# Storing the last tiles of a linear-attention and MLP kernel: one two-batch transfer from SyncE's queue in place of two half transfers from two queues

## The chip, the cores and the metric

The kernel runs on one core of a Trainium2 chip. The metric is the device time of one execution in microseconds; lower is better. The kernel before takes 283.94 us, the median of three runs that lie between 283.93 and 284.04. A profiled execution took 283.87 us, and the traced part of it, the span, is 282.1 us long. All times below that are positions in the trace are counted from the start of that span.

## The reference, cut to what matters

```python
B, H, S, D = 8, 8, 576, 64          # batches, heads, sequence, head size
q, k, v: (B, H, S, D) float32       # about N(0, 0.1)
w_in: (512, 2048)    w_out: (2048, 512)

phi(x)  = where(x > 0, x, exp(x) - 1) + 1
kv      = einsum('bhsd,bhse->bhde', phi(k), v)
z       = sum over s of phi(k)
attn    = (phi(q) @ kv) / (phi(q) @ z + 1e-6)
x       = attn as (B*S, H*D) = (4608, 512)
out     = gelu_tanh(x @ w_in) @ w_out      # (4608, 512) float32
```

The output has 4608 rows of 512 float32, which is 2048 bytes per row. Batch b owns rows 576 b to 576 b + 575.

## The kernel before

A batch has 576 rows, which is four tiles of 128 and a rest of 64. The kernel runs the MLP for each batch on its first 512 rows (`MAIN`), in iterations 0 to 7. The 64 rows left over from each of the eight batches (`REST`) are collected, two batches to a tile, into four tiles of 128 rows. Iteration 8 (`j == B`) runs the MLP on them. So a tile `t` of the rest group holds 64 rows of batch 2t in partitions 0 to 63, and 64 rows of batch 2t + 1 in partitions 64 to 127. In the output these two blocks of 64 rows lie 576 rows apart.

In iterations 0 to 7, two tiles at a time are stored in one transfer from ScalarE's queue, with 128 partitions of 1024 float32. In iteration 8 each tile is evacuated from PSUM by VectorE or ScalarE in turn, and stored by two transfers, one for each batch. The last tile is computed in three column pieces of 256, 128 and 128, each with its own evacuation and its own two stores.

```python
P = 128; MAIN = 512; REST = S - MAIN          # REST = 64
pout = tile_pool(name="pout", bufs=2)         # two o_sb buffers, used in turn
# ... (cut)

def store_rest(t, o_sb, fs, engs):
    for s in range(2):
        r0 = (2 * t + s) * S + MAIN
        engs[s].dma_start(
            out=out[r0 : r0 + REST, fs], in_=o_sb[REST * s : REST * (s + 1), 0, fs]
        )

def finish(j, t, o_ps):
    if j == B:                                 # the rest group
        o_sb = pout.tile([P, 2, d_model], FP32, name="o_sb")
        evac(o_sb[:, 0, :], o_ps, t % 2)       # VectorE for even t, ScalarE for odd t
        store_rest(t, o_sb, slice(0, d_model), (nc.scalar, nc.sync))
        return
    # ... (cut: iterations 0 to 7, one store of two tiles from ScalarE's queue:)
    #     ov = out[j*S : j*S+MAIN].rearrange("(p c) f -> p c f", c=C)[:, t-1 : t+1]
    #     nc.scalar.dma_start(out=ov, in_=o_sb)

def last_tile(g, t):                           # t = 3 of the rest group
    o_sb = pout.tile([P, 2, d_model], FP32, name="o_sb")
    for n, fs in enumerate((slice(0, 256), slice(256, 384), slice(384, d_model))):
        o_ps = bank("o_ps", [P, fs.stop - fs.start])
        o_mm(o_ps, g, t, range(MM), fs)
        evac(o_sb[:, 0, fs], o_ps, n == 0)     # ScalarE, then VectorE twice
        store_rest(t, o_sb, fs, (nc.scalar, nc.sync))
```

Of the kernel before, what the change touches and what calls it, by code (L numbers as in the profile page):

```python
# [15 lines left out]
def kernel(  # L16
# [16 lines left out]
    nc = tc.nc  # L33

    B, H, S, D = q.shape
    d_model, d_ff = moe_w_in.shape
# [3 lines left out]
    MAIN = P * C  # L40
    REST = S - MAIN
# [37 lines left out]
    def bank(name, shape, dt=FP32):  # L79
        return ps_b.tile(shape, dt, name=name, tag="b")  # L80
# [421 lines left out]
    def at(j, slot, fn, *args):  # L502


        fill.setdefault((j, slot), []).append((fn, args))
# [179 lines left out]
    def evac(dst, src, on_scalar):  # L685
        (nc.scalar.copy if on_scalar else nc.vector.tensor_copy)(dst, src)  # L686

    def store_rest(t, o_sb, fs, engs):
        for s in range(2):
            r0 = (2 * t + s) * S + MAIN  # L690
            engs[s].dma_start(
                out=out[r0 : r0 + REST, fs], in_=o_sb[REST * s : REST * (s + 1), 0, fs]
            )

    o_sbs = {}

    def finish(j, t, o_ps):
        if j == B:
            o_sb = pout.tile([P, 2, d_model], FP32, name="o_sb")
            evac(o_sb[:, 0, :], o_ps, t % 2)  # L700
            store_rest(t, o_sb, slice(0, d_model), (nc.scalar, nc.sync))
            return
        if t % 2 == 0:
            o_sbs[j, t // 2] = pout.tile([P, 2, d_model], FP32, name="o_sb")
        o_sb = o_sbs[j, t // 2]
        if j == 0 and t in (1, 2):
            at(0, 35, evac, o_sb[:, t % 2, :], o_ps, True)
        else:
            evac(o_sb[:, t % 2, :], o_ps, t < C - 1 if j == 0 else t % 2)
        if t % 2 == 1:  # L710
            ov = out[j * S : j * S + MAIN, :].rearrange("(p c) f -> p c f", c=C)[:, t - 1 : t + 1]

            def store():
                nc.scalar.dma_start(out=ov, in_=o_sb)

            if j == 0:
                at(1, 2, store)
            else:
                store()

    def o_mm(o_ps, g, t, ms, fs=slice(0, d_model), half=None):
        for m in ms:
            if m == ms.start + 2 and half:
                run(*half)
            nc.tensor.matmul(  # L725
                o_ps,
                lhsT=g[:, m, P * t : P * (t + 1)],
                rhs=w_out_sb[:, m, fs],
                start=(m == 0),
                stop=(m == MM - 1),  # L730
            )

    def last_tile(g, t):
        o_sb = pout.tile([P, 2, d_model], FP32, name="o_sb")
        for n, fs in enumerate((slice(0, 256), slice(256, 384), slice(384, d_model))):
            o_ps = bank("o_ps", [P, fs.stop - fs.start])
            o_mm(o_ps, g, t, range(MM), fs)
            evac(o_sb[:, 0, fs], o_ps, n == 0)
            store_rest(t, o_sb, fs, (nc.scalar, nc.sync))

    def iteration(j):
        xt = xts[j] if j < B else xt_rest
# [12 lines left out]
        for slot, step in enumerate(steps):  # L755
            if step[0] == "h":
                m = step[1]
                h_ps = h_begun.get(j, {}).get(m)
                if h_ps is None:
                    h_ps = bank("h_ps", [P, MAIN])  # L760
                    h_mm(h_ps, xt, m)
                gelu(g, m, h_ps)
            else:
                t, u = step[1:]
                if j == B and t == C - 1:
                    if u.start == 0:
                        last_tile(g, t)
                    continue
                if u.start == 0:
                    o_pss[t] = bank("o_ps", [P, d_model])  # L770
                o_mm(o_pss[t], g, t, u, half=(j, slot - 0.5))
                if u.stop == MM:
                    finish(j, t, o_pss[t])
            run(j, slot)
# [54 lines left out]
```

## Time and profile before

| What | Value | From |
|---|---|---|
| Time, median of three | 283.94 us | the runs |
| Span of the trace | 282.1 us | the profile page |
| PE busy | 276.1 us, 98% | the page, part 1 |
| ACT, DVE, POOL busy | 164.3, 102.6, 15.0 us | the page, part 1 |
| Granted TensorE clock | 0.998 on average | the run |
| Output stores of iterations 0 to 7 | 16 of 512 KB from ScalarE's queue, 3.2 us to landing | the page, part 6 |
| Output stores of the rest group | 12, six from each queue, 128 KB to 32 KB, from 269.1 to 279.1 us | the trace, by line L691 |

PE stands for TensorE's matmuls, DVE for VectorE, ACT for ScalarE, POOL for GpSimd. SPq and ACTq are the instruction streams of SyncE and ScalarE in which transfers are issued. Lines such as L691 are lines of the kernel. In the DMA views q1 is the queue of transfers that SyncE issues and q10 that of transfers that ScalarE issues; this follows from their counts and sizes. A packet is one piece of a transfer as one of the core's 16 DMA engines moved it. "Share of 16 engines" is the sum of the packets' times over 16 times the length of the window. "Landing" is counted from the issue of a transfer to its last completion event.

### The profile page before, as it was taken

The page shows a single profiled execution, that of the slowest core. Times are in us where ns is not written, and L with a number is a line of the kernel's source. Part 1 is how long each engine was busy: PE and PEld are TensorE (multiplying, and loading weights), DVE is VectorE, ACT ScalarE, POOL GpSimd, SP SyncE. Part 2 cuts the span into 40 slices and gives each one's busy share as a digit, 9 for nine tenths or more (in the row PEclk, how much of TensorE's full clock was granted, in tenths as well). Part 3 has the DMA queues.
Part 4 walks back from the last instruction along what each step waited for, and adds up shares of the span by engine and source line. Part 5 has one row for each costly group of instructions (what it writes and reads, how often), then busy time and mean ns, then how long its engine had stood idle before and what let it go on. Part 6 is the DMA issues. An engine that isn't in the chain of part 4 may idle for free.

```text
span 282.1 us, 5465 instructions
## 1 busy us (share of the span) xinstructions
PE 276.1 (98%) x2341; PEld 135.3 (48%) x2341; DVE 102.6 (36%) x177; ACT 164.3 (58%) x224; POOL 15.0 (5%) x21
## 2 busy tenths in 40 slices
PE   8899999999999999999999999999999999999995
PEld 3474455445444544454445444544444444444444
DVE  3850386344955750356034640350124001400001
ACT  4678878786986905692569346833681364026400
POOL 3147210000000000000000000000000000000000
PEclk9999999999999999999999999999999999999999
DMA  7999999978899767916794740056405300520022
GB/s 245 401 406 397 410 402 404 404 251 222 185 379 294 263 153 212 380 26 168 188 388 114 151 131 0 2 151 168 94 2 149 114 0 2 142 81 0 2 74 74
DMA packets 59591, 53.83 MB, mean 191 GB/s; under 512 B 35760, under 2 KB 45360, under 8 KB 59568
## 3 DMA queue, kind: packets, MB, share of 16 engines
q1 hardware_dynamic: 56784, 44.58, 51.0%
q10 hardware_dynamic: 2784, 8.91, 8.7%
q8 instruction: 18, 0.29, 0.4%
q14 instruction: 5, 0.04, 0.0%
HBM read 36.70 MB, written 9.44 MB: 164 GB/s over the span
## 4 chain that ended last, share of the span: by engine, by line
PE 94%; DMA 3%; SPq 1%; DVE 1%; issue 0%; ACT 0%
PE o_ps L725 44%; PE h_ps L384 44%; DMA v_x<-in_v_dram 3%; PE n_ps L322 1%; PE n_ps L249 1%; PE kv_ps L249 1%; PE n_ps L265 1%; PE t_ps L377 1%; SPq L95 1%; SPq L100 0%; PE t_ps L530 0%; DVE vp L238 0%; DVE x L367 0%; DVE kvbd L261 0%; DVE o_sb L686 0%
## 5 line engine op out<-in xcount | busy, mean ns | idle before, releaser
L725 PE MATMUL o_ps<-w_out_sb,g 128*128 128x512 bf16 (+2 forms) x608 | 128.4, 368 | 0.0
L384 PE MATMUL h_ps<-xt,w_in_sb 128*128 128x512 bf16 (+1 forms) x564 | 113.7, 359 | 0.0
L394 ACT ACTIVATE g<-h_ps 128x512 bf16<-128x512 f32 x144 | 84.5, 599 | 36.4 <-PE h_ps L384 35.1
L384 PEld LDWEIGHTS <-w_in_sb 128*128 128x128 bf16 x628 | 58.5, 98 | 64.7
L725 PEld LDWEIGHTS <-g 128*128 128x128 bf16 x608 | 57.4, 98 | 63.5
L686 ACT COPY o_sb<-o_ps 128x512 f32<-128x512 f32 (+1 forms) x19 | 10.8, 576 | 65.7 <-PE o_ps L725 58.9
L686 DVE COPY o_sb<-o_ps 128x512 f32<-128x512 f32 (+1 forms) x19 | 12.2, 645 | 50.5 <-PE o_ps L725 45.6
L282 DVE RECIPROCAL r<-n_ps 128x6 f32<-128x6 f32 (+2 forms) x43 | 8.2, 191 | 60.9 <-PE n_ps L322 55.4
L227 DVE TENSOR_SCALAR k_p<-k_x 128x2304 bf16<-128x2304 f32 (+1 forms) x9 | 11.0, 1222 | 24.4 <-DMA k_x<-in_k_dram 24.4
L283 DVE TENSOR_TENSOR xs<-n_ps,r 128x384 bf16<-128x384 f32 (+1 forms) x30 | 17.5, 584 | 1.0
L219 ACT ACTIVATE k_e<-k_x 128x2304 bf16<-128x2304 f32 (+1 forms) x9 | 17.1, 1902 | 0.9 <-DMA k_x<-in_k_dram 0.8
L219 ACT ACTIVATE q_e<-q_x 128x2048 bf16<-128x2048 f32 (+1 forms) x9 | 15.5, 1719 | 2.8 <-DMA q_x<-in_q_dram 2.7
L227 DVE TENSOR_SCALAR q_p<-q_x 128x2048 bf16<-128x2048 f32 (+1 forms) x9 | 9.9, 1102 | 13.1 <-DMA q_x<-in_q_dram 13.1
L384 PE MATMUL h_ps<-xt_rest,w_in_sb 128*128 128x512 bf16 x64 | 14.0, 379 | 0.0
L233 DVE TENSOR_TENSOR q_p<-q_p,q_e 128x2048 bf16<-128x2048 bf16 (+1 forms) x9 | 9.9, 1100 | 6.9 <-ACT q_e L219 6.8
L407 ACT ACT_TABLE_LOAD x9 | 11.5, 1283 | 0.2
L233 DVE TENSOR_TENSOR k_p<-k_p,k_e 128x2304 bf16<-128x2304 bf16 (+1 forms) x9 | 11.0, 1221 | 1.2 <-ACT k_e L219 1.0
L238 DVE CAST vp<-v_x 128x2304 bf16<-128x2304 f32 (+1 forms) x9 | 11.0, 1223 | 0.5 <-DMA v_x<-in_v_dram 0.4
L416 PE MATMUL w_ps<-warm 128*128 128x512 bf16 x32 | 9.3, 445 | 1.2 <-DVE warm L181 1.2
L219 ACT ACT_TABLE_LOAD x8 | 10.3, 1283 | 0.1
L139 POOL CAST w_in_sb<-w_st 128x512 bf16<-128x512 f32 (+2 forms) x6 | 7.6, 1271 | 14.6 <-DMA w_st<-in_moe_w_in_dram 14.6
L283 DVE TENSOR_TENSOR x<-n_ps,r 128x512 bf16<-128x512 f32 (+1 forms) x13 | 7.9, 609 | 0.4
(50 smaller groups left out, 77.5 us busy)
## 6 DMA issues: line engine op xcount, KB each, us to landing
out_dram<-o_sb ACTq DMA_DIRECT2D x16, 512.0 KB, 3.2
k_x<-in_k_dram SPq DMA_DIRECT2D x7, 1152.0 KB, 7.2
v_x<-in_v_dram SPq DMA_DIRECT2D x7, 1152.0 KB, 11.8
q_x<-in_q_dram SPq DMA_DIRECT2D x6, 1024.0 KB, 9.6
w_st<-in_moe_w_in_dram SPq DMA_DIRECT2D x3, 1024.0 KB, 13.5
q_x<-in_q_dram SPq DMA_DIRECT2D x4, 512.0 KB, 8.5
w_st<-in_moe_w_out_dram SPq DMA_DIRECT2D x2, 1024.0 KB, 12.5
w_st<-in_moe_w_out_dram SPq DMA_DIRECT2D x4, 512.0 KB, 11.2
```

The source lines that it names most:

```text
L219: nc.scalar.activation(o, i, AF.Exp)
L227: nc.vector.tensor_scalar(o, i, 1.0, 1.0, op0=ALU.add, op1=ALU.max)
L233: nc.vector.tensor_tensor(p, p, e, op=ALU.min)
L238: fn(out=vp_paired(b)[:, :, us, 0:D].rearrange("p j u d -> p u j d"), in_=ld["v", b][:, us].rearrange("p u (j d) -> p u j d", d=D),)
L282: nc.vector.reciprocal(r, n_v[heads + (D,)])
L283: nc.vector.tensor_tensor(x_v, n_v[heads + (slice(0, D),)], r[heads + (None,)].to_broadcast(shape + [D]), op=ALU.mult,)
L384: nc.tensor.matmul(h_ps[:, ts], lhsT=w_in_sb[:, c, P * m : P * (m + 1)], rhs=xt[:, c, ts], start=(c == 0), stop=(c == KM - 1), skip_group_ ...
L394: nc.scalar.activation(g[:, m, :], h_ps, AF.Gelu_apprx_tanh)
L407: nc.scalar.preload_act_table_set("gelu_apprx_tanh_and_others")
L416: nc.tensor.matmul(w_ps, lhsT=warm[:, 0:P], rhs=warm)
L686: (nc.scalar.copy if on_scalar else nc.vector.tensor_copy)(dst, src)
L725: nc.tensor.matmul(o_ps, lhsT=g[:, m, P * t : P * (t + 1)], rhs=w_out_sb[:, m, fs], start=(m == 0), stop=(m == MM - 1),)
```

## The change

`store_rest` is rewritten. In place of a loop over the two batches, which issues one transfer of 64 partitions for each from two queues, there is a single transfer of all 128 partitions from SyncE's queue. Its destination is the output seen as batches by rows, two batches and the last 64 rows of each, so that the step between the two batches is a dimension of the access pattern. The aim is fewer issued transfers: six in place of twelve, and none of them on ScalarE's instruction stream.

```diff
-    def store_rest(t, o_sb, fs, engs):
-        for s in range(2):
-            r0 = (2 * t + s) * S + MAIN
-            engs[s].dma_start(
-                out=out[r0 : r0 + REST, fs], in_=o_sb[REST * s : REST * (s + 1), 0, fs]
-            )
+    def store_rest(t, o_sb, fs, eng):
+
+        eng.dma_start(
+            out=out.rearrange("(b s) f -> b s f", s=S)[2 * t : 2 * t + 2, MAIN:S, fs],
+            in_=o_sb[:, 0, fs],
+        )
 ... (finish)
-            store_rest(t, o_sb, slice(0, d_model), (nc.scalar, nc.sync))
+            store_rest(t, o_sb, slice(0, d_model), nc.sync)
 ... (last_tile)
-            store_rest(t, o_sb, fs, (nc.scalar, nc.sync))
+            store_rest(t, o_sb, fs, nc.sync)
```

Nothing else moves: the order of the instructions on TensorE, VectorE and GpSimd is the same in both programs, and ScalarE's and SyncE's differ only in these stores. In the built program the destination of a full tile's store has the counts 2 x 64 x 512 (outermost first), with steps of 294912, 512 and 1 elements; its source has 128 partitions of 512 elements. The stores of before have 64 x 512 on both sides.

## The prediction

> **What bounds the kernel now.** I read the page's chain first, then the chain's last stretch, then the tail in order of time, and last the DMA packets in windows of it. The chain, from the page (shares of the span by engine):
>
> ```profile
> ## 4 chain that ended last, share of the span: by engine, by line
> PE 94%; DMA 3%; SPq 1%; DVE 1%; issue 0%; ACT 0%
> ```
>
> TensorE sets the time, and no output store is on the chain. A change to stores can only matter behind TensorE's last matmul. The chain from 250 us on (start us, us, what):
>
> ```profile
> 264.80 13.91 PE o_ps L725 x96
> 278.70 0.02 issue
> 278.73 0.29 DVE o_sb L686
> ```
>
> The chain of working instructions ends with the last evacuation at 279.02 us. The span ends at 282.1. So 3.1 us of the end is the last stores, which the chain doesn't count. The tail in order of time (start us, us, stream, line, operation):
>
> ```profile
> 264.63 14.06 PE L725 MATMUL o_ps<-w_out_sb,g 128*128 128x512 bf16 x96
> ...
> 268.34 0.69 DVE L686 COPY o_sb<-o_ps 128x512 f32<-128x512 f32 x1 [20.03 <-PE o_ps L725]
> 269.06 10.45 SPq L691 DMA_DIRECT2D out_dram<-o_sb  x6
> 269.06 0.56 ACTq L691 DMA_DIRECT2D out_dram<-o_sb  x1
> 271.74 0.59 ACT L686 COPY o_sb<-o_ps 128x512 f32<-128x512 f32 x1 [6.31 <-PE o_ps L725]
> ...
> 275.19 0.69 DVE L686 COPY o_sb<-o_ps 128x512 f32<-128x512 f32 x1 [6.16 <-PE o_ps L725]
> 276.94 0.37 ACT L686 COPY o_sb<-o_ps 128x256 f32<-128x256 f32 x1 [4.61 <-PE o_ps L725]
> ...
> 277.89 0.29 DVE L686 COPY o_sb<-o_ps 128x128 f32<-128x128 f32 x1 [2.00 <-PE o_ps L725]
> 278.73 0.29 DVE L686 COPY o_sb<-o_ps 128x128 f32<-128x128 f32 x1 [0.55 <-PE o_ps L725]
> ```
>
> The reader is to see the rhythm: stores become ready at 269.06, 272.36 and about 275.9 (full tiles, 256 KB each), then 277.34, 278.2 and 279.02 (the pieces of the last tile). One full tile comes every 3.4 us. Now how fast the stores move. First the DMA of the window 269.0 to 272.3 us, the first tile alone, 64 rows of 2 KB on each queue; then that of 252.2 to 254.2, a store of iteration 7 alone, 128 rows of 4 KB (queue, packets, MB, share of 16 engines):
>
> ```profile
> q1 hardware_dynamic: 80, 0.13, 17.9%
> q10 hardware_dynamic: 80, 0.13, 10.5%
> ```
>
> ```profile
> q10 hardware_dynamic: 144, 0.52, 63.9%
> ```
>
> Each store of before has 64 or 128 row packets and 16 tiny ones: one completion from each of 16 engines. In the packet records a completion takes 9 ns. So a 2 KB row that isn't mixed with another queue's took (0.105 x 16 x 3.3 us - 16 x 9 ns) / 64 = 84 ns of one engine, and a 4 KB row (0.639 x 16 x 2.0 us - 16 x 9 ns) / 128 = 159 ns. That is about 9 ns and 75 ns for each 2 KB: one engine moves some 24 GB/s, and speed comes from 16 of them at once. In the packet records of the last tile a row of 1 KB takes 44 ns at least and one of 512 B 27 ns in the middle, which fits.
>
> **What the Trainium skill says.** Its page "DMA: Bandwidth & Descriptors", section "Why a DMA increments its semaphore by 16 and not by 1", says how many engines k a transfer is spread over: k is the largest number up to 16 that divides the outermost count (of those that aren't 1) of both access patterns; only those k engines post a completion and the issuing sequencer makes up the rest. The section "Rules for kernel authors" warns that an outermost dimension of size c below 16 confines the whole transfer to at most c engines, and wants a multiple of 16 outermost. The trace agrees as far as it goes: every store of before has 64 or 128 outermost and shows 16 completion packets. No transfer of before has a smaller outermost count, so no run shows the small k yet. The section "Issuing engines are not separate DMA queues" says that transfers from different queues share the same 16 engines and two queues save only issuing time. The trace agrees: while both queues ran, q1's mean row took 145 ns (9.45 us less 0.14, over 64), far above 84.
>
> **The change part by part.**
>
> 1. Removed: six issues on ScalarE's stream, of 0.49 to 0.56 us each. ScalarE waits for TensorE there for 4.6 to 6.3 us at a time, so this gives nothing.
> 2. The last store of before is ScalarE's, issued at 279.1; SyncE's was at 279.0. One transfer with 16 engines would have its last row about 0.3 us earlier (the last q1 row ended at 280.47, the last q10 row at 280.74). This is the most that the change can gain.
> 3. The spread: the new destination is 2 x 64 x 512. The outermost counts are 2 and 128, so by the rule k = 2. Each tile then goes out on two engines, 64 rows on each, and all six stores take the same two engines (by the page, the lowest-numbered ones).
>    - a full tile: 64 x 84 ns = 5.4 us (before: 1.1 us from first row to last, 270.27 to 271.38);
>    - the 256-column piece: 64 x 45 ns = 2.9 us;
>    - each 128-column piece: 64 x 27 ns = 1.7 us.
>    Sum: 3 x 5.4 + 2.9 + 2 x 1.7 = 22.5 us of work on each of the two engines.
> 4. When they start: in before the first row moved at 270.27, 1.2 us after the issue at 269.06. That stays. A tile comes every 3.4 us and takes 5.4, so from then on the two engines always have work: 270.3 to 275.6, 281.0, 286.4 (three full tiles), 289.3, 291.0, 292.8.
> 5. The end: in before the span ended 1.35 us after the last row (280.74 to 282.09). So the span ends at 292.8 + 1.35 = 294.1, which is 12.0 us later.
>
> All of these 12 us lie behind TensorE's last matmul, where nothing runs beside them. 283.94 + 12.0 = 295.9 us, 4.2% slower.
>
> **The rivals.**
>
> - *All 16 engines take part*, because the hardware or the sequencer reshapes the pattern, or takes k from the source's 128 partitions. Then step 2 alone remains, and the time is 283.6 us, within the noise of nothing. For it: the source does have 128 partitions, the bytes and rows are the same, and nothing in before shows k below 16. Against it: the stated rule, which names both sides. I give this 12%.
> - *The store buffers become a wait.* `pout` has two buffers, so the third tile's evacuation needs the first tile's store landed, and the last tile's needs the second's. With two engines the first store lands about 276.0, against 275.19 when VectorE is ready; the second about 281.4, against 276.94. So both evacuations will wait, the second for over 4 us. Does it cost? The third store would then be issued at about 276.0 + 0.7 = 276.7 and its rows could start at 278; the engines are busy until 281.0. The last tile's first piece would be issued at 281.4 + 0.4 = 281.8 and could start at 283; the engines are busy until 286.4. So there is a new wait with 3 us of slack, and it adds nothing unless landing takes much longer than the 0.4 us after the last row that I take from before. If it did not hide, each tile would add some 2 us: 298 to 300.
> - *The rate of a lone engine differs.* Rows that follow one another on one engine with 14 others silent might go faster than 84 ns (less traffic) or slower (the wait for the write of 2 KB shows when one engine must do it all). 10% either way is 2.2 us. The 4 KB stores ran back to back at 159 ns with all 16 busy, so I hold the rate to be the engine's own.
> - *SyncE's queue stalls while issuing.* 64 rows for each engine in place of 4 might fill what holds pending rows, and SyncE's issues would stretch from 0.47 us to several. It has no other work there, so the engines still get rows in order; no change of time.
>
> **Range and chances.** With two engines, the terms that can move are the rate (295.9 less or more 2.2) and the small pieces (64 x 62 ns, the middle of the records where both queues ran, in place of 45 would add 1.1). I take 293.0 to 298.5. The 16-engine rival is a separate peak near 283.6 that I leave outside the range. Chances: 0.86 slower by over 2% (above 289.6), which is k = 2 with nearly any rate; 0.12 within 2%; 0.02 faster, for which I see no way, since at most 0.3 us of 283.94 can be gained.
>
> **What would show it.** Step 3: in the window of the tail, 64 row packets per engine and only two completions for a transfer, thus 130 packets for a full tile in place of 160; a DMA share of about 2/16 = 12.5% flat from 270.3 to the end, at about 48 GB/s; landing of about 7 us for the first tile (269.06 to 276.0) and 8 to 11 for the later ones, in place of 1.8 to 2.7. Step 4: no gap in that flat stretch. Step 5: TensorE's last matmul still at 278.7, and the span ending at about 294. The buffer rival: VectorE and ScalarE waiting for the DMA of out_dram before their copies in the last 20 us. I am wrong if the DMA share in the tail peaks well above 2/16, if the stretch of stores is much shorter than 22 us, or if TensorE's end moves.

## The result and the profile after

The changed kernel takes 296.05 us, the median of six runs between 295.99 and 296.14. Beside it the kernel before took 283.9. The ratio is 1.0428 with a 95% interval of 1.0414 to 1.0441: it is 4.3% slower. The predicted time was 295.9 us and the range 293.0 to 298.5.

First the chain on the page of the kernel after (shares of the span):

```profile
## 4 chain that ended last, share of the span: by engine, by line
PE 88%; DMA 6%; SPq 1%; DVE 1%; ACT 0%; issue 0%; DVEq 0%
```

TensorE was 94% of it and is 88% now, and transfers have gone from 3% to 6%. TensorE itself does the same work: 276.1 us busy in both. The end of the chain shows what has come in (start us, us, what):

```profile
264.77 6.92 PE o_ps L725 x32
271.70 0.02 issue
271.72 0.59 ACT o_sb L686
272.31 0.02 issue
272.33 9.99 DMA out_dram<-o_sb
...
282.51 0.29 DVE o_sb L686
282.80 0.20 DVEq L824
```

The chain leaves TensorE after its second tile, and passes through the second tile's store for 10 us to the last evacuations. It ends at 283.0, and the span at 294.2: the last 11.2 us are again stores, which the chain doesn't count. The tail in order of time:

```profile
264.61 14.06 PE L725 MATMUL o_ps<-w_out_sb,g 128*128 128x512 bf16 x96
...
268.32 0.69 DVE L686 COPY o_sb<-o_ps 128x512 f32<-128x512 f32 x1 [20.03 <-PE o_ps L725]
269.04 18.58 SPq L690 DMA_DIRECT2D out_dram<-o_sb  x6
271.72 0.58 ACT L686 COPY o_sb<-o_ps 128x512 f32<-128x512 f32 x1 [6.31 <-PE o_ps L725]
277.32 0.69 DVE L686 COPY o_sb<-o_ps 128x512 f32<-128x512 f32 x1 [8.31 <-DMA out_dram<-o_sb]
282.42 0.37 ACT L686 COPY o_sb<-o_ps 128x256 f32<-128x256 f32 x1 [10.12 <-DMA out_dram<-o_sb]
282.51 0.49 DVE L686 COPY o_sb<-o_ps 128x128 f32<-128x128 f32 x2 [4.50 <-DMA out_dram<-o_sb]
```

TensorE's last matmul ends at 278.7, as before. The first two evacuations come as before. The third and the last waited for a store to land, and no longer for TensorE. SyncE's six issues are spread over 18.6 us in place of 10.5.

Now the DMA of the tail: the busy tenths of the 16 engines in 40 slices, and the packets, of the window from 269 us to the end. First the kernel before, then the kernel after:

```profile
DMA  0001978000000297900000003995076240330000
...
DMA packets 960, 1.05 MB, mean 80 GB/s; under 512 B 192, under 2 KB 576, under 8 KB 960
```

```profile
DMA  0011111011111111111111111111111111111100
...
DMA packets 780, 1.05 MB, mean 42 GB/s; under 512 B 12, under 2 KB 396, under 8 KB 780
...
q1 hardware_dynamic: 780, 1.05, 11.9%
```

The same 1.05 MB and the same 768 rows, but short bursts of up to 9 tenths have become a flat line of one tenth. The packets under 512 B are the completions, since no row is smaller than 512 B. There were 192 of them for 12 stores, 16 for each. Now there are 12 for six stores, two for each. So two of the 16 engines carried every store.

### The profile page after: what moved, and what is told of

It is laid out like the page before. It is cut to its first block, busy times and chain, and to the rows that moved or that the text cites. A ratio compares the mean times of both kernels' runs of the same rounds, so it can differ in the third digit from the quotient of the medians.

```text
span 294.2 us, 5454 instructions
## 1 busy us (share of the span) xinstructions
PE 276.1 (94%) x2341; PEld 135.2 (46%) x2341; DVE 102.6 (35%) x177; ACT 164.3 (56%) x224; POOL 15.0 (5%) x21
## 4 chain that ended last, share of the span: by engine, by line
PE 88%; DMA 6%; SPq 1%; DVE 1%; ACT 0%; issue 0%; DVEq 0%
PE h_ps L384 42%; PE o_ps L725 40%; DMA out_dram<-o_sb 3%; DMA v_x<-in_v_dram 3%; PE n_ps L322 1%; PE n_ps L249 1%; PE kv_ps L249 1%; PE n_ps L265 1%; PE t_ps L377 1%; SPq L95 1%; SPq L100 0%; PE t_ps L530 0%; DVE vp L238 0%; ACT o_sb L686 0%; DVE x L367 0%
## 5 line engine op out<-in xcount | busy, mean ns | idle before, releaser
L219 ACT ACT_TABLE_LOAD x8 | 10.3, 1283 | 0.1
## 6 DMA issues: line engine op xcount, KB each, us to landing
q_x<-in_q_dram SPq DMA_DIRECT2D x4, 512.0 KB, 11.4
```

The source lines that it names most:

```text
L219: nc.scalar.activation(o, i, AF.Exp)
```

## The experiments

The ratio and its interval compare each run with the kernel before on the same chip. That kernel took 284.31 us beside e_two_sp, e_rows_outer, e_outer4 and e_outer8, 284.30 beside e_t0_halves, and 283.86 beside the other runs. The expected times start from 283.9, so for the first five of these runs it is better to compare losses than times.

| Run | Outermost counts (destination, source) | Time, us | Ratio to before, 95% interval |
|---|---|---|---|
| The changed kernel | 2, 128 | 296.05 | 1.0428 (1.0414 to 1.0441) |
| e_two_sp | 64, 64 | 285.5 | 1.0042 (1.003 to 1.0055) |
| e_rows_outer | 64, 128 | 284.25 | 0.9994 (0.9986 to 1.0002) |
| e_outer4 | 4, 128 | 287.77 | 1.0123 (1.0108 to 1.0138) |
| e_outer8 | 8, 128 | 284.74 | 1.0016 (1.001 to 1.0023) |
| e_own_bufs | 2, 128 | 296.07 | 1.0427 (1.0409 to 1.0444) |
| e_alt_queues | 2, 128 | 296.14 | 1.043 (1.0415 to 1.0446) |
| e_last_only | 2, 128 in the last tile | 288.11 | 1.0147 (1.013 to 1.0164) |
| e_full_only | 2, 128 in the full tiles | 291.57 | 1.0268 (1.0253 to 1.0284) |
| e_t0_halves | 2, 128 from the second tile on | 294.34 | 1.0355 (1.0338 to 1.0372) |

The theory is that the outermost count of 2 confines each store to two DMA engines, and that the two engines' backlog is the whole loss. The rivals are that one queue in place of two costs the time, that a transfer with a step between batches or one transfer in place of two does, and that the wait for output buffers does.

### One queue, nothing else: e_two_sp

```diff
-            store_rest(t, o_sb, slice(0, d_model), (nc.scalar, nc.sync))
+            store_rest(t, o_sb, slice(0, d_model), (nc.sync, nc.sync))
...
-            store_rest(t, o_sb, fs, (nc.scalar, nc.sync))
+            store_rest(t, o_sb, fs, (nc.sync, nc.sync))
```

(against the kernel before)

> The two half transfers of before stay (64 rows outermost on both sides), but both are issued from SyncE's queue. Spread theory (two DMA engines because the outermost count is 2): the outermost counts are still 64, so all 16 engines work, and the time stays at 283.9, plus up to 0.4 us for the second half's later issue: 283.9 to 284.4, 160 packets for a full tile. One-queue theory (the loss comes from giving up ScalarE's queue and sending 1 MB through one queue): 290 to 296.

It took 285.5 us, beside 284.31 for the kernel before: 1.2 us lost, a tenth of what the change lost, and 0.8 more than I had allowed. Giving up ScalarE's queue is not the cause, but it isn't free with 12 issues. SyncE's issues by the line of the store (ns minimum, median, maximum; first and last start), in e_two_sp:

```profile
L691 SPq DMA_DIRECT2D out_dram<-o_sb x12: 466/567/590, 269.4 to 280.8; - x12
```

Each issue holds SyncE for about 0.6 us, so the two halves of a piece take 1.2 us, while in before the last three stores became ready at 277.34, 278.21 and 279.05. The issues ran late: those of the two last pieces started at 278.88, 279.48, 280.15 and 280.75, the last 1.7 us after the last of before. Of this, 0.3 us is a shift of the whole tail (TensorE's last matmul ended at 278.99 in place of 278.69), and 1.4 us is delay. I had counted one extra issue and not that they add up over the pieces.

### The same single transfer with the rows outermost: e_rows_outer

```diff
     def store_rest(t, o_sb, fs, eng):
 
         eng.dma_start(
-            out=out.rearrange("(b s) f -> b s f", s=S)[2 * t : 2 * t + 2, MAIN:S, fs],
+            out=out.rearrange("(b s) f -> s b f", s=S)[MAIN:S, 2 * t : 2 * t + 2, fs],
             in_=o_sb[:, 0, fs],
         )
...
+    def gelu_rows(g, m, h_ps):         # the rest group only
+        nc.scalar.activation(
+            g[:, m, :].rearrange("p (t s b) -> p t b s", t=C, b=2),
+            h_ps.rearrange("p (t b s) -> p t b s", t=C, b=2),
+            AF.Gelu_apprx_tanh,
+        )
```

(against the changed kernel)

> One transfer for a tile from SyncE's queue with a step between the two batches, as in the changed kernel, but the destination's dimensions are 64 rows x 2 batches x 512 in place of 2 x 64 x 512; for that the Gelu of the rest group writes its columns in the order row, batch, so that partition 2r + b holds row r of batch b. Same bytes, same 128 rows, same number of transfers, same queue. Spread theory: outermost counts 64 and 128, so 16 engines, 144 packets for a full tile, and 283.6 to 284.0. Rival (a transfer with a step between batches, or one transfer for the tile, or one queue, is what costs): about 296.

It took 284.25 us, and the ratio to the kernel before is 0.9994 (0.9986 to 1.0002). Its time is 0.25 us above the expected range, but so was that of the kernel before. The entire loss is gone, with one queue, six transfers and a step between the batches all kept. Only the order of the destination's dimensions differs, and with it the order of rows in a tile and that in which the Gelu writes them. The DMA of its tail, in the same view as above:

```profile
DMA  0000089100000019800000000791028060320000
...
DMA packets 864, 1.05 MB, mean 78 GB/s; under 512 B 96, under 2 KB 480, under 8 KB 864
```

The bursts are back, and there are 96 completions for six stores, 16 for each. The reordered Gelu itself, by shape (busy us, mean ns):

```profile
L397 ACT ACTIVATE g<-h_ps 128x512 bf16<-128x512 f32 x16 | 11.9, 743 | 2.1 <-PE h_ps L384 0.4
```

Writing every second element costs ScalarE 743 ns in place of about 600, which stays inside TensorE's rhythm of 0.86 us for a column block (the Gelus of before start that far apart) and so costs no time here.

### Four and eight outermost: e_outer4 and e_outer8

```diff
         eng.dma_start(
-            out=out.rearrange("(b s) f -> s b f", s=S)[MAIN:S, 2 * t : 2 * t + 2, fs],
+            out=out.rearrange("(b s) f -> b s f", s=S)[
+                4 * (t % 2) : 4 * (t % 2 + 1), MAIN + 32 * (t // 2) : MAIN + 32 * (t // 2 + 1), fs
+            ],
             in_=o_sb[:, 0, fs],
         )
```

(e_outer4 against e_rows_outer, with the Gelu's columns ordered to match; in e_outer8 a tile holds 16 rows of all eight batches)

> As e_rows_outer, but the columns are ordered so that a tile holds 32 rows of each of four batches, and the destination is 4 x 32 x 512. Spread theory: 4 engines, 32 rows each, 132 packets for a full tile. At the row cadence of the changed kernel (80, 42 and 24 ns) a full tile takes 2.6 us, less than the 3.4 us between tiles, so hardly a backlog: third tile 277.1 to 279.7, the pieces to 281.0, 281.8 and 282.5, end of the span 283.9, time 285.7 (285.0 to 286.5). Rival (the step or the one transfer costs, whatever the outermost count): about 296.

> As e_outer4 with 16 rows of each of eight batches, destination 8 x 16 x 512. Spread theory: 8 engines, 16 rows each, 136 packets for a full tile; a full tile takes 1.3 us, no backlog, last piece 280.2 to 280.6, time 283.6 to 284.1. Rival: about 296.

They took 287.77 and 284.74 us. The DMA of the tail, first of e_outer4, then of e_outer8:

```profile
DMA  0001222122222312222224012222222222220000
...
DMA packets 792, 1.05 MB, mean 63 GB/s; under 512 B 24, under 2 KB 408, under 8 KB 792
```

```profile
DMA  0000344344400054434500006433544455410000
...
DMA packets 816, 1.05 MB, mean 75 GB/s; under 512 B 48, under 2 KB 432, under 8 KB 816
```

Completions for each store are 4 and 8, and where the stores run, the share is mostly 2 tenths with four engines (4/16 is 25%) and 4 or 5 with eight. So over 2, 4, 8 and 64 outermost the engines are 2, 4, 8 and 16, and the losses against before 12.2, 3.5, 0.4 and -0.1 us. The rule about the engines holds at each point; the source's count was 128 in all four, so its part in the rule isn't tested. But e_outer4 lost 1.7 us more than the 1.8 that I expected, though the count of engines was right. The packet records show why: its full tiles took 4.1, 3.2 and 3.6 us on their four engines in place of 2.6, so a backlog formed all the same. In e_outer8 each of the three took 2.3 in place of 1.3, and the loss of 0.4 us is more than the 0.2 that I had allowed. The difference comes from single slow rows early in each transfer: single packets took up to 860 ns in e_outer4 and 475 in e_outer8, where most took 84 (see e_t0_halves).

### Buffers of their own: e_own_bufs

```diff
+    prest = ctx.enter_context(tc.tile_pool(name="prest", bufs=3))
...
         if j == B:
-            o_sb = pout.tile([P, 2, d_model], FP32, name="o_sb")
+            o_sb = prest.tile([P, 1, d_model], FP32, name="o_sr")
```

(against the changed kernel)

> The changed kernel, but the first three tiles of the rest group have three output buffers of their own, so that no evacuation waits for a store. Spread theory: the waits of VectorE and ScalarE for the stores (8.3 and 10.1 us) go away, all six stores are issued by 279.1, and the time stays: 295.7 to 296.3, because the two DMA engines never run empty. Rival (the buffers' wait is part of the loss): 291 to 294.

> The same kernel as e_own_bufs, for a profile (that run's profiled execution was a disturbed one of 1029 us, its timed ones were 295.9 to 296.1). Spread theory: no wait of VectorE or ScalarE for the DMA of out_dram, the last evacuation at 279.0, and the rows of the stores without a gap from 270.3 to 292.9 all the same; span about 294.2. Rival (the buffers' wait is part of the loss): the last row ends well before 292.

It took 296.07 us, the ratio 1.0427, no different from the changed kernel; one of its four executions, of 1029 us, was disturbed and is left out. The execution of e_own_bufs2, from which the trace is, took 296.31. Who waited for whom in the tail of the changed kernel, and then in that of e_own_bufs2 (us in total, times, longest):

```profile
...
DVE o_sb L686 <- DMA out_dram<-o_sb: 12.8, 2, 8.3
ACT o_sb L686 <- DMA out_dram<-o_sb: 10.1, 1, 10.1
...
```

```profile
DVE o_sr L687 <- PE o_ps L726: 26.2, 2, 20.0
ACT o_sr L687 <- PE o_ps L726: 6.3, 1, 6.3
ACT o_sb L687 <- PE o_ps L726: 4.6, 1, 4.6
DVE o_sb L687 <- PE o_ps L726: 2.5, 2, 2.0
...
```

The waits for stores are gone altogether, the last evacuation starts at 279.07, and the rows still run without a gap from 270.61 to 293.16. The new wait of up to 10.1 us stood on the chain of the changed kernel and cost nothing. SyncE then blocked instead: in e_own_bufs2 its last three issues held it 1.8, 5.0 and 3.3 us.

### Two queues again: e_alt_queues

```diff
-            store_rest(t, o_sb, slice(0, d_model), nc.sync)
+            store_rest(t, o_sb, slice(0, d_model), (nc.sync, nc.scalar)[t % 2])
...
-            store_rest(t, o_sb, fs, nc.sync)
+            store_rest(t, o_sb, fs, (nc.scalar, nc.sync)[n % 2])
```

(against the changed kernel)

> The changed kernel's two-batch transfers, issued in turn from SyncE's and ScalarE's queues. Spread theory: both queues' transfers run on the same two DMA engines, so the sum of 22 us of rows stays and with it the time: 296 to 296.8. One-queue theory: two queues halve it, 288 to 291.

It took 296.14 us. The DMA queues of its tail:

```profile
q1 hardware_dynamic: 390, 0.59, 6.6%
q10 hardware_dynamic: 390, 0.46, 4.8%
```

The two queues together have 11.4% of the 16 engines over this window, where two engines busy throughout would have 12.5%. The rows ran from 270.47 to 293.05, 22.6 us as in the changed kernel. Both queues' stores ran on one pair. In the packet records, ScalarE's first store, issued at 272.50, moved its first row only at 276.68, shortly before the last row of SyncE's at 277.38. Two of the later pieces, one from each queue, did mix (286.98 to 291.39 and 287.47 to 291.63), and each took about as long as the two together would have in a row: 4.4 and 4.2 us, against 2.73 and 1.52 alone in the changed kernel. The second queue added no engine here, and no store finished ahead of one issued before it.

### Part of the change: e_last_only and e_full_only

Both have `store_halves`, which is the old `store_rest`, beside the new one.

```diff
-            store_rest(t, o_sb, slice(0, d_model), nc.sync)                # e_last_only
+            store_halves(t, o_sb, slice(0, d_model), (nc.scalar, nc.sync))
...
-            store_rest(t, o_sb, fs, nc.sync)                               # e_full_only
+            store_halves(t, o_sb, fs, (nc.scalar, nc.sync))
```

(each of the two edits alone, against the changed kernel)

> Only the three pieces of the last tile are stored by one two-batch transfer each; the three full tiles keep the two half transfers of before. Spread theory: no backlog of full tiles; the pieces start at 278.5 and take 64 x (42 + 24 + 24) ns = 5.8 us on two engines, last row 284.2, span 285.6, time 287.4 (287 to 288.7). Rival (a fixed cost for each such transfer, 12.1 us over six): 290.

> Only the three full tiles are stored by one two-batch transfer each; the last tile's pieces keep the two half transfers. Spread theory: the two engines are busy with the full tiles until 287.1 as in the changed kernel; the halves that SyncE issues stand behind them on these two engines and take 4 rows each there, last row about 287.5, span 288.9, time 290.7 (290 to 291.5). If only the buffers' wait counted (the last tile's evacuation at 282.4): issue of the last piece at 284.3, span 287.3, time 289.1.

They took 288.11 and 291.57 us, with 283.86 for the kernel before. The two losses, 4.25 and 7.71 us, add up to 11.96, close to the whole loss of 12.15 us (296.05 less 283.9). A backlog that is a sum of row times should add up like this. e_full_only came out just above the stated 290 to 291.5, and its last row at 288.22 in place of 287.5. A fixed cost for each two-batch transfer would have made the two equal, at about 290 us; the three full tiles, with three times the bytes, cost 1.8 times what the three pieces did. They didn't cost three times as much because part of their rows moved while TensorE was still working; only what sticks out behind its last matmul counts.

### Which transfer pays the slow start: e_t0_halves

```diff
-            store_rest(t, o_sb, slice(0, d_model), nc.sync)
+            if t == 0:
+                store_halves(t, o_sb, slice(0, d_model), (nc.scalar, nc.sync))
+            else:
+                store_rest(t, o_sb, slice(0, d_model), nc.sync)
```

(against the changed kernel)

> The changed kernel, but the first full tile goes out as two half transfers on 16 engines; the second is then the first two-batch transfer. In the changed kernel the first full tile took 6.6 us on its two engines and the next two, which followed without a gap, 5.1 each. Theory 'the extra 1.4 us is paid by a transfer that finds its engines idle': the second tile takes 6.6 us (273.6 to 280.2), the third 5.1, the pieces 5.8, last row 291.1, span 292.4, time 294.2. Rival 'the extra time belongs to the first store of the rest group, whatever it is': 5.1 for the second, time 292.8.

It took 294.34 us, 10.0 more than the kernel before; the theory had 10.3 and the rival 8.9. In the packet records the second tile took 6.5 us (273.89 to 280.39) and the third, which followed without a gap, 5.1 (280.38 to 285.51). So the extra 1.4 us isn't tied to the first store of the rest group; it moved to the first two-batch store. The DMA of the second tile's window and then of the third's shows the holes at the start:

```profile
DMA  0102011012012012021011111111111111111110
```

```profile
DMA  1101111011110111101111011110111101101011
```

That the engines were idle before is not what makes the slow rows, though, as this run alone would let one think. In e_outer4 the second and third tile came right behind the one before (first rows at 274.51 and 277.68, last rows of the tile before ended at 274.57 and 277.75), and both had slow rows. What these stores have in common with the first is that they had been issued only 2.1 and 1.7 us before their first row. Nearly all slow rows of the full tiles start within 4.3 us of the store's issue on two engines, within 3.2 on four and within 2.4 on eight. The second and third tile of the changed kernel, whose first rows came 4.5 and 3.9 us after their issue, have none. So among these stores, slow rows go with a recent issue; no run varies that alone.

## Why the prediction was right

**The bound.** Right. TensorE's work and its end (278.7) didn't move, and everything added lies after it.

**Steps 1 and 2, the small gains.** Right in size. e_rows_outer has everything that these steps count on (six issues, none on ScalarE, 16 engines) and gains nothing measurable, though the interval leaves room for the 0.3 us. The issues that went were not waited for, and the last one, behind the last evacuation, is there in both. One reading of step 2 was rounding: the last two stores of before were both issued at 279.05, so the 0.3 us between their last rows did not come from a later issue.

**Step 3, two engines.** Right, shown by two completions a store and by the runs with 4, 8 and 64 outermost. e_rows_outer isolates it: the order of the destination's dimensions alone returns the loss. The Trainium skill's page "DMA: Bandwidth & Descriptors", section "Why a DMA increments its semaphore by 16 and not by 1", had the rule, and these runs agree with it at 2, 4, 8 and 16 engines, with the destination's count varied and the source's left at 128.

The sum of step 3 was right for a partly wrong reason. Its terms against the packet records of the changed kernel:

| Term | Predicted, us | Measured, us |
|---|---|---|
| First full tile | 5.4 | 6.57 |
| Second and third full tile | 5.4 each | 5.14 each |
| Piece of 256 columns | 2.9 | 2.73 |
| Two pieces of 128 columns | 1.7 each | 1.52 each |
| Sum | 22.5 | 22.6 |

I took the time of a packet (84 ns) for the distance between two. Packets on one engine overlap a little: 5.14 us over 64 rows is 80 ns. And I had no term for the slow rows of a store that reaches its engines soon after its issue. Without slow rows the sum would have been 3 x 5.14 + 2.73 + 2 x 1.52 = 21.2 us, so the first error made me 1.3 us too high, and the missing term (6.57 less 5.14) 1.4 us too low. They cancel in the changed kernel, and that the time came out within 0.2 us is luck to this extent. They don't cancel in e_outer4, where the loss was 1.7 us above what I expected.

**Steps 4 and 5, no gap and the end.** Right. The first row moved at 270.30, 1.26 us after its issue; the rows ran on to 292.85; the span ended 1.36 us later, at 294.2 where I had 294.1.

**The rivals.** The 16-engine rival fell. The buffer rival was right as a wait and right in costing nothing: VectorE waited until 277.32 and ScalarE until 282.42 (I had said 276.0 and 281.4, 1.3 and 1.0 us early, for want of the 1.4 us that the first store's slow rows add), and e_own_bufs removes the wait without moving the time. The lone engine's rate was the engine's own within 5%. SyncE did stall: its last issue took 3.28 us in place of 0.5, at no cost.

**A reading that was wrong.** For the statement that two queues share the engines, I gave as evidence that q1's rows took 145 ns in the first tile of before, "while both queues ran". That evidence doesn't hold. In e_two_sp, with one queue alone, the 2 KB rows of the half transfers take 140 ns too, and in before 45 of q1's 64 rows of that tile were over before q10's began (270.27 to 271.05 against 270.85 on). So the other queue is not what these rows waited for; what it was stays open. The statement itself is borne out by e_alt_queues.

**Landing times.** I said the landing of the stores would rise to between 7 and 11 us. The views of the kernel after give no landing for these stores; the waits of the evacuations stand in for it: the first store was issued at 269.04 and VectorE released at 277.32, 8.3 us later where I had 7. In the packet records the last completions came 7.0 to 9.7 us after the issues of the six stores.

## What to carry to other kernels

Before two transfers are merged into one with a step, look at their outermost counts: here the destination's set how many DMA engines work, and a batch dimension of 2 in front cut 16 to 2. Put the dimension with many rows outermost, if need be by changing the order in which an earlier operation writes its columns; with that the merged store was as fast as the two it replaced. And ask first what a saved issue is worth: with stores behind the last matmul, the time to move the last bytes counts, and issues that nothing waits for bring nothing.

## What the runs showed that I had not expected

- Stores on 2, 4 and 8 engines that reach them soon after their issue have slow rows at first: the first 256 KB store took 6.6 us on two engines where later ones took 5.1, 4.1 in place of 2.6 on four, and 2.3 in place of 1.3 on eight. In the changed kernel 16 of the first store's 128 rows took over 90 ns, up to 508, all in its first 3.4 us. The single stores on 16 engines in e_rows_outer, issued as recently and on idle engines, had no row over 84 ns, while half stores of 64 rows on 16 engines (before, e_two_sp) took a mean of up to 154 ns a row. What these rows wait for stays open.
- A single issue held SyncE for up to 5.0 us in e_own_bufs2, with earlier stores still waiting for the two engines; its first three issues took 0.5 to 0.7.
- Twelve half stores from one queue cost 1.2 us (e_two_sp), through issues that ran 1.4 us late, because the pieces of the last tile come faster (0.85 us) than two issues of 0.6 us.
